# Three edits in a fused attention and mixture-of-experts kernel: operands of a late matmul stage swapped, experts in another order, one scaling on another engine

## The chip, the cores and the metric

The kernel runs on one core of a Trainium2 chip. The metric is the device time of one execution in microseconds. TensorE is called PE, VectorE DVE, ScalarE ACT, GpSimd POOL and SyncE SP, as in the profile. SP, ACT and POOL have queues on which they issue DMAs.

## The reference

Three layers follow one another. Matrices are float32; the kernel splits each operand into a high and a low part (`hi`, `lo`) and takes three matmuls for one product (`mm3`: hi·hi, hi·lo, lo·hi).

```python
# attention: 4 batches, 8 heads, 576 positions, 64 columns, causal with decay
attn = softmax(q @ k.T / 8 + cum[i] - cum[j], causal) ; x = attn @ v   # x: 2304 x 512
# mixture of experts: 8 experts, 512 -> 1024 -> 512
en = emb / (norm(emb) + 1e-6) ; logits = xn @ en.T / tau
e = argmax(logits) ; gate = softmax(logits)[e]
y[e == k] = gate * (relu(x[e == k] @ w1[k]) @ w2[k])
# second layer: 512 -> 3 x 768 -> 512
h = maximum(maximum(y @ m1, y @ m2), y @ m3) ; out = h @ mo
```

With the reference's inputs (seed 0) the eight experts get 360, 313, 312, 305, 292, 250, 244 and 228 tokens. The one with 305 has 232 of them in the first three batches, which makes it the third largest there.

## The kernel before

The order of the instructions on every engine is written out when the kernel is built: a list scheduler (`Sched`, line 146) takes tasks with an engine or a choice of engines, an assumed cost, dependences and a priority, and always emits the task that can begin first by its own estimates. Tasks hold buffers by name (`get`, `rel`). Each engine then works through its list in order, with semaphores between them. So an estimate changed in one place can move instructions in another.

**Attention** (`attention`, line 259) takes 16 pairs of heads in turn: scores, masked maximum on DVE, `exp` on ACT, transposes of the probabilities on PE, the product with v, and a matmul with `w144` (line 568) that also gives each head's share of the expert logits. `expert_rows` (line 112) makes the columns of `w144` from the scaled expert embeddings: a short chain over DVE and POOL for the norms (lines 118 to 127), a scaling of 8x512 on DVE (line 129), four transposes (line 133) and two copies (line 137). `route_batch` (line 779) picks the expert of each token of a batch. The 64 KB pieces of x go to `x_dram` by line 588; the last pair's pieces go out on SP's and ACT's queues in turn.

**The early expert.** After three batches `early_expert` (line 838) chooses the expert that is third by size so far (`SEAT`). Its first 256 tokens (`SOON`) are gathered, and `early_slot` (line 609) computes h = relu(x·w1) for them at the end of attention: eight chunks of 128 rows of w1, 12 matmuls of 256 columns each (`pe`, lines 679 to 698, called through `mm3`, lines 1172 to 1174), into three PSUM buffers. The weights w1 are loaded in four pieces (line 657), the third into a part of the v buffer, the fourth when the first's input tile is free. `square_sums` (line 939) runs five squares for each batch on ACT (line 943).

**The late tokens.** Up to 96 tokens (`LATE`) of that expert come from the last batch. `first_slot` (line 887) finds them, POOL gathers them (line 1336), PE transposes them (line 1343) and ACT and DVE split them (lines 1209 and 1354). In `moe` (line 1177), expert 0's pass over `hmm` then takes 96 matmuls with the weights as the stationary side and the 96 tokens as the moving side:

```python
for kc in range(KC):
    mm3(nc, ph[:, 0:C], w[0][:, kc, fs], w[1][:, kc, fs], X[k][0][:, kc, 0:C], X[k][1][:, kc, 0:C], kc == 0, kc == KC - 1)
```

The results go through relu (line 1406) and a subtraction (line 1411) into columns of the same h tiles (`g.he`). Then `ymm` multiplies h (340 columns) by w2 in 96 matmuls (`py`).

**The other experts.** `sort_experts` (line 975) sorts them by size, the early one first; slot k has room for `CAP[k]` tokens and is `CAP[k]` columns wide in both matmul stages (`ph`, `py`, 96 matmuls each). Its tokens are gathered in chunks of up to 128. Weights arrive in pieces of 512 KB (line 1239), are split by ACT (line 1209) and DVE (line 1226) and live in a ring of four. Beside the experts, weights of the second layer are decoded on DVE (lines 1269 to 1294). Tokens that don't fit a slot are done in a loop at the end of the program. The **second layer** works through 2304 columns in five chunks.

Of the kernel before, what the change touches and what calls it, by code (L numbers as in the profile page):

```python
# [19 lines left out]
DW = D + E  # L20
# [10 lines left out]
CAP = [340, 384, 338, 316, 298, 280, 264, 244]  # L31
# [6 lines left out]
NCOL = 24  # L38
CHUNKS = [(0, 384), (384, 512), (896, 512), (1408, 512), (1920, 384)]
# [72 lines left out]
def expert_rows(nc, g, sp, ps):  # L112
# [11 lines left out]
    nc.vector.scalar_tensor_tensor(out=ss[:, 2:3], in0=ss[:, 0:1], scalar=ss[:, 2:3], in1=ss[:, 1:2], op0=ALU.mult, op1=ALU.add)  # L124
# [3 lines left out]
    yield dict(eng="DVE", cost=0.65)  # L128
    nc.vector.tensor_scalar(out=e, in0=e, scalar1=ss[:, 3:4], scalar2=rt, op0=ALU.mult, op1=ALU.mult)
# [129 lines left out]
def attention(tc, g, qT, kT, v, x_dram, es):  # L259
# [266 lines left out]
    def pair_out(p):  # L526
# [63 lines left out]
        sd.task("SP", 3.2, store, u0, [fn_[p, 0], fn_[p, 1]], lat=2.0)  # L590
# [8 lines left out]
    def batch_out(b):  # L599
# [3 lines left out]
        last[0] = sd.chain(g.batch_done(b, lg), pr, deps + [last[0], consts_done] + ([part[0], part["pick"]] if b == B - 1 else []))  # L603
        sd.chain(g.square_sums(b, lambda: XL[b][:, :, :, 0:D]), pr + 40, deps + [consts_done])
# [4 lines left out]
    def early_slot(chosen):  # L609
# [6 lines left out]
        wdone, xdone, xhis, wl = [], [], [], []  # L616

        for c in range(SOON // 128):
# [26 lines left out]
            th = sd.task(("ACT", "DVE"), (act(512), dve(512)), xhi, 10 * NP + 15, [tr] + ready[NP - 1])  # L645
            xhis.append(th)
            xdone.append(sd.task("DVE", dve(512), xlo, 10 * NP + 15, [th], rel=[("s", ("xe", c))]))

        for q in range(4):
            def load(e, q=q):  # L650
                if not er:
                    er[0] = nc.sync.value_load(g.expi0[0:1, 0:1], min_val=0, max_val=E - 1)
                if q == 2:
                    raw[q] = V[0].rearrange("p a d -> p (a d)")[:, 0:1024]
                else:
                    raw[q] = flat(ld.tile([128, 2, S], F32, tag=("q2", "k2")[q % 2], name=f"we{q}"))[:, 0:1024]
# [11 lines left out]
            when = scores_of(NP - 3) if q < 2 else scores_of(NP - 2) + xhis + (late if q == 2 else [fn_[NP - 1, 1]])  # L668
            u = 10 * NP + (20, 21, 22, 31.2)[q]
            free = [chosen] + ready[NP - 2] if q < 2 else [chosen, fo[NP - 5]] if q == 2 else [wdone[1], xhis[0]]  # L670
            l = sd.task("SP", 1.5, load, 10 * NP - 12 + q, free, lat=3.0)
# [6 lines left out]
        for f in range(8):  # L678
            def mm(e, f=f):
                t = ph[f] = ps_s.tile([128, 512], F32, tag="s", name=f"pe{f}")  # L680
# [21 lines left out]
            m = sd.task("PE", 12 * (SOON + 31) / 2400, mm, u, [wdone[f // 2], fbs[NP - 1, 0], fbs[NP - 1, 1]] + xdone, get=("s", ("e", f)))  # L702
            th = sd.task(("ACT", "DVE"), (act(SOON), dve(SOON)), relu, u, [m])
            sd.task("DVE", dve(SOON), rest, u, [th], rel=[("s", ("e", f))])

    last, part, fbs = [None], {}, {}
# [19 lines left out]
    early_slot(part["pick"])  # L726
# [7 lines left out]
def routing_consts(nc, g, cp):  # L734
# [9 lines left out]
    g.iok = iota("iok", [128, E, E], [[1, E], [0, E]])  # L744
# [34 lines left out]
def route_batch(nc, g, b, lg, rp, ps):  # L779
# [22 lines left out]
                                   op1=ALU.is_equal)  # L802
    yield dict(eng="PE", cost=0.2, get=("o", ("pr", b)))
# [9 lines left out]
    if last:  # L813
        yield from first_slot(nc, g, b, pr, rp, ps)
        return
# [22 lines left out]
def early_expert(nc, g, cp, rp, ps):  # L838
    EE, ST = [128, E, E], [128, NCH, E]
    step, two = dict(eng="DVE", cost=0.24, kind="port"), dict(eng="DVE", cost=0.4, kind="port")  # L840
# [4 lines left out]
    yield two  # L845
    key = rp.tile([128, E], F32, tag="key", name="key3")
    nc.vector.scalar_tensor_tensor(out=key, in0=p3[:, 0:E], scalar=8.0, in1=g.w8[:, 1, :], op0=ALU.mult, op1=ALU.add)
    cnt = rp.tile([128, E], F32, tag="cnt", name="cnt3")
    nc.vector.tensor_copy(cnt, p3[:, 0:E])
    yield dict(eng="DVE", cost=0.24, kind="port", rel=[("o", "p3")])  # L850
    gt = rp.tile(EE, F32, tag="gt", name="gt3")
    nc.vector.tensor_tensor(out=gt, in0=key.unsqueeze(1).to_broadcast(EE), in1=key.unsqueeze(2).to_broadcast(EE), op=ALU.is_gt)
    yield two
    r = rp.tile([128, E], F32, tag="r", name="r3")
    nc.vector.tensor_reduce(out=r, in_=gt, op=ALU.add, axis=AX.X)
    g.ohe = cp.tile([128, E], F32, name="ohe")
    nc.vector.tensor_scalar(out=g.ohe, in0=r, scalar1=float(SEAT), scalar2=None, op0=ALU.is_equal)
    yield two
    ex = rp.tile([128, E], F32, tag="ex", name="ex")
    nc.vector.tensor_tensor(out=ex, in0=g.ohe, in1=g.ioe[:, 0, :], op=ALU.mult)  # L860
    g.expi0 = cp.tile([128, 1], I32, name="expi0")
    with low(reason="an expert's number, summed in float32, is a small whole number"):
        nc.vector.tensor_reduce(out=g.expi0, in_=ex, op=ALU.add, axis=AX.X)
    yield two
    tm = rp.tile(ST, F32, tag="tm", name="tm")
    nc.vector.tensor_tensor(out=tm, in0=g.tab.rearrange("p e c -> p c e"), in1=g.ohe.unsqueeze(1).to_broadcast(ST), op=ALU.mult)
    tab0 = rp.tile([128, NCH], F32, tag="tab0", name="tab0")
    nc.vector.tensor_reduce(out=tab0, in_=tm, op=ALU.add, axis=AX.X)
# [887 lines left out]
```

## Time and profile before

| what | value |
|---|---|
| three runs | 751.6, 751.2, 755.11 us; median 751.6 |
| profiled execution, its own time | 753.75 us |
| its span, first to last instruction | 752.0 us, so 1.75 us lie around it |
| granted PE clock, mean over the span | 0.983 of full speed |
| PE busy | 733.8 us (98%) |
| DVE, ACT, POOL busy | 445.0, 371.2, 143.6 us |

PE's busy time counts each matmul from its begin to its modelled end, and matmuls overlap; how fast PE works is read from the distance between two begins. [...]

### The profile page before, as it was taken

To read this page: it belongs to the slowest core of one execution; us is meant where nothing else is said; L and a number is where in the kernel's file an instruction comes from. 1 tells how busy PE (TensorE), PEld (TensorE's weight loads), DVE (VectorE), ACT (ScalarE), POOL (GpSimd) and SP (SyncE) were. 2 spreads that over 40 slices of the span, in tenths; PEclk is the share of its full clock that TensorE was granted. 3 is DMA by queue.
4 is the path that set the end of the run, shared out by engine and by line. 5 is a ranking of instruction groups with operands and counts; after the bars stand their busy time and mean duration, and the time that the engine had idled before them with its cause. 6 is when DMAs were issued, how large, how long until landed. Compare 5 with 4: busy or idle time off the path is not lost. (4 is left out here: it accounts for less than half of the span.)

```text
span 752.0 us, 13022 instructions
## 1 busy us (share of the span) xinstructions
PE 733.8 (98%) x4743; PEld 666.0 (89%) x4743; DVE 445.0 (59%) x1131; ACT 371.2 (49%) x850; POOL 143.6 (19%) x145
## 2 busy tenths in 40 slices
PE   8899999999999999999989999999999999999996
PEld 8788888887899999999989999988888888888995
DVE  8988878988755888888677879612212231221220
ACT  7689989988537554556555554411121121112111
POOL 6966364541011100110210000010020001001001
PEclk9999999999978999999999999999999999999999
DMA  7868657534434565556657543010010001001001
GB/s 250 252 185 253 190 159 192 137 88 145 140 113 141 176 202 197 194 169 236 225 170 233 167 160 128 13 43 1 0 43 14 1 15 42 1 1 42 15 1 44
DMA packets 44731, 89.78 MB, mean 119 GB/s; under 512 B 23280, under 2 KB 23280, under 8 KB 44664
## 3 DMA queue, kind: packets, MB, share of 16 engines
q1 hardware_dynamic: 40536, 78.97, 33.8%
q0 software_dynamic: 3552, 9.80, 3.7%
q8 instruction: 39, 0.64, 0.4%
q14 instruction: 28, 0.23, 0.1%
q10 hardware_dynamic: 576, 0.15, 0.1%
HBM read 74.89 MB, written 9.44 MB: 112 GB/s over the span
## 5 line engine op out<-in xcount | busy, mean ns | idle before, releaser
L1526 DVE TENSOR_TENSOR tm<-pm,tm 128x512 f32<-128x512 f32 (+1 forms) x60 | 38.3, 638 | 184.6 <-PE pm L1174 184.5
L1172 PE MATMUL pm<-y,m 128*128 128x512 f32 (+1 forms) x288 | 109.4, 380 | 0.0
L1173 PE MATMUL pm<-y,m 128*128 128x512 f32 (+1 forms) x288 | 109.4, 380 | 0.0
L1174 PE MATMUL pm<-y,m 128*128 128x512 f32 (+1 forms) x288 | 109.4, 380 | 0.0
L466 ACT ACTIVATE P<-P,nm 128x576 f32<-128x576 f32 (+2 forms) x144 | 83.6, 584 | 6.4 <-DVE nm L442 5.0
L1226 DVE TENSOR_TENSOR w<-stg,w 128x1024 fp32r<-128x1024 f32 x60 | 73.3, 1221 | 19.5 <-ACT w L1209 19.1
L1568 POOL DMA_INDIRECT out_dram<-oo,ctidx x18 | 17.8, 987 | 336.6 <-ACT oo L1565 333.6
L1209 ACT ACTIVATE g<-tm 128x512 fp32r<-128x512 f32 (+1 forms) x30 | 17.7, 589 | 118.4 <-DVE tm L1526 118.4
L1209 ACT ACTIVATE w<-stg 128x1024 fp32r<-128x1024 f32 x58 | 61.0, 1055 | 27.4 <-issue 9.8
L1172 PE MATMUL py<-h,w 128*128 128x384 f32 (+6 forms) x224 | 69.4, 310 | 0.0
L1174 PE MATMUL py<-h,w 128*128 128x384 f32 (+6 forms) x224 | 68.3, 305 | 0.0
L1173 PE MATMUL py<-h,w 128*128 128x384 f32 (+6 forms) x224 | 68.2, 305 | 0.0
L1172 PE MATMUL ph<-x,w 128*128 128x384 f32 (+6 forms) x224 | 67.9, 303 | 0.0
L1173 PE MATMUL ph<-x,w 128*128 128x384 f32 (+6 forms) x224 | 67.6, 302 | 0.0
L1174 PE MATMUL ph<-x,w 128*128 128x384 f32 (+6 forms) x224 | 67.6, 302 | 0.0
L414 PE MATMUL s<-R,At 128*128 128x288 f32 (+3 forms) x170 | 60.6, 370 | 3.1 <-DVE nm L442 1.2
L1172 PEld LDWEIGHTS pm<-y,m 128*128 128x128 f32 x288 | 54.2, 188 | 9.4
L1173 PEld LDWEIGHTS pm<-y,m 128*128 128x128 f32 x288 | 54.2, 188 | 9.4
L1174 PEld LDWEIGHTS pm<-y,m 128*128 128x128 f32 x288 | 54.2, 188 | 9.4
L442 DVE CUSTOM_DVE_ANT_0 P<-s,mask 128x288 f32<-128x288 f32 (+3 forms) x128 | 58.3, 475 | 3.2 <-PE s L420 1.4
L1336 POOL DMA_INDIRECT gat<-x_dram,gidx x21 | 23.4, 1116 | 190.0 <-PE xt L1343 148.2
L485 PE MATMUL t<-ident,P 128*128 128x128 f32 x320 | 56.7, 277 | 0.8 <-ACT PT L524 0.3
(369 smaller groups left out, 1799.5 us busy)
## 6 DMA issues: line engine op xcount, KB each, us to landing
stg<-in_w_dram SPq DMA_DIRECT2D x60, 512.0 KB
sd<-in_m_dram SPq DMA_DIRECT2D x18, 512.0 KB
q<-in_q_dram SPq DMA_DIRECT2D x15, 576.0 KB
k<-in_k_dram SPq DMA_DIRECT2D x15, 576.0 KB
Bt<-At SPq DMA_DIRECT2D x15, 288.0 KB
V<-in_v_dram SPq DMA_DIRECT2D x4, 1024.0 KB
x_dram<-XL SPq DMA_DIRECT2D x62, 64.0 KB
sd_o<-in_mo_dram SPq DMA_DIRECT2D x6, 512.0 KB
```

What stands on the lines that cost most here:

```text
L414: nc.tensor.matmul(st[:, 0:wp], lt[0:kk, r, q0:q0 + 128], rt[0:kk, r, j0:j0 + wp], start=(ps_i == 0), stop=(p > 0 and ps_i == 1))
L442: nc.vector.tensor_tensor_reduce(out=P[0:n, j0:j0 + w], in0=st_.pop((h, t, k))[0:n, 0:w], in1=g.mask[0:n, m0:m0 + w], scale=-0.125, scalar ...
L466: nc.scalar.activation(out=P[0:n, 0:ext], in_=P[0:n, 0:ext], func=AF.Exp, bias=nm[0:n, k:k + 1], scale=-1.0, accum_out=sums[b][0:n, t, c:c ...
L485: nc.tensor.transpose(w[:, 128 * a:128 * a + 128], P[:, 128 * a:128 * a + 128], g.ident)
L1172: nc.tensor.matmul(out, whi, xhi, start=start, stop=False)
L1173: nc.tensor.matmul(out, whi, xlo, start=False, stop=False)
L1174: nc.tensor.matmul(out, wlo, xhi, start=False, stop=stop)
L1209: nc.scalar.activation(out=out, in_=in_, func=AF.Copy)
L1226: ENG[e].tensor_tensor(out=w[:, 1], in0=t, in1=w[:, 0].bitcast(F32), op=ALU.subtract)
L1336: nc.gpsimd.indirect_dma_start(out=t[0:n], out_offset=None, in_=x_dram, in_offset=bass.IndirectOffsetOnAxis(ap=idx, axis=0))
L1526: nc.vector.tensor_tensor(out=mx[0], in0=mx["p", w][:, 0:MC], in1=mx[0], op=ALU.max)
L1568: nc.gpsimd.indirect_dma_start(out=out, out_offset=bass.IndirectOffsetOnAxis(ap=g.sidx[:, col:col + 1], axis=0), in_=o[1], in_offset=None, ...
```

## The change

The first expert's pass over h gets code of its own, `late_rows`: in four quarters of 256 columns of w1, the 96 tokens are the stationary side and the weights the moving side, 12 matmuls a quarter. The result stands tokens by columns, so each quarter goes through relu, two transposes on PE, a copy and a subtraction into the h tiles. `CAP` is in another order, with 256 where 264 was, and `RANK` says which size belongs to which slot. The expert rows are scaled on ACT with one factor, and one step of their norm is a `tensor_scalar`. At the end of attention: the last pair's five stores all go out on SP; the last batch's squares follow the third early chunk; the early chunks alternate between two PSUM pools (five buffers) and their relu is always on ACT; the third and fourth weight pieces go into a spare `XL` tile; `early_expert`'s counts become a task of their own (`early_count`), and the late tokens' ids (`late_ids`) are made ahead of the ranks' matmuls. A gather's assumed cost and delay are 1.27 and 2.9 for 1.04 and 2.4; sorting waits for the first half of the token split alone.

```diff
-CAP = [340, 384, 338, 316, 298, 280, 264, 244]
+CAP = [340, 338, 256, 384, 244, 316, 280, 298]
+RANK = [0] + [1 + sorted(CAP[1:], reverse=True).index(c) for c in CAP[1:]]
# expert_rows
-    nc.vector.scalar_tensor_tensor(out=ss[:, 2:3], in0=ss[:, 0:1], scalar=ss[:, 2:3], in1=ss[:, 1:2], op0=ALU.mult, op1=ALU.add)
+    nc.vector.tensor_scalar(out=ss[:, 2:3], in0=ss[:, 0:1], scalar1=ss[:, 2:3], scalar2=ss[:, 1:2], op0=ALU.mult, op1=ALU.add)
...
-    yield dict(eng="DVE", cost=0.65)
-    nc.vector.tensor_scalar(out=e, in0=e, scalar1=ss[:, 3:4], scalar2=rt, op0=ALU.mult, op1=ALU.mult)
+    nc.vector.tensor_scalar(out=rt, in0=rt, scalar1=ss[:, 3:4], scalar2=None, op0=ALU.mult)
+    yield dict(eng="ACT", cost=0.65)
+    nc.scalar.activation(out=e, in_=e, func=AF.Copy, scale=rt)
# attention
-                (nc.scalar if p == NP - 1 and t % 2 else nc.sync).dma_start(out=dst[r0:r0 + ROWS[t]], in_=X[0:ROWS[t], t])
+                nc.sync.dma_start(out=dst[r0:r0 + ROWS[t]], in_=X[0:ROWS[t], t])
-                if q == 2:
-                    raw[q] = V[0].rearrange("p a d -> p (a d)")[:, 0:1024]
+                if q > 1:
+                    if q == 2:
+                        raw["x"] = xl.tile([128, NBLK, H, DW], F32, tag="XL", name="spare").rearrange("p t h c -> p (t h c)")
+                    raw[q] = raw["x"][:, 1024 * (q - 2):1024 * (q - 1)]
-                t = ph[f] = ps_s.tile([128, 512], F32, tag="s", name=f"pe{f}")
+                t = ph[f] = (ps_t if f % 2 else ps_s).tile([128, 512], F32, tag="st"[f % 2], name=f"pe{f}")
-            th = sd.task(("ACT", "DVE"), (act(SOON), dve(SOON)), relu, u, [m])
+            th = sd.task("ACT", act(SOON), relu, u, [m])
+    sd.chain(g.square_sums(B - 1, lambda: XL[B - 1][:, :, :, 0:D]), 10 * NP + 60, [mains[2]])
# routing_consts
-    g.iok = iota("iok", [128, E, E], [[1, E], [0, E]])
+    g.iok = cp.tile([128, E, E], F32, name="iok")
+    for k in range(E):
+        nc.gpsimd.memset(g.iok[:, k], float(RANK[k]))
# moe
-            ga = sd.task("Pool", 1.04, gather, use - 12, deps, get=("scr", (k, c)), lat=2.4)
+            ga = sd.task("Pool", 1.27, gather, use - 12, deps, get=("scr", (k, c)), lat=2.9)
-    sorted_ = sd.chain(sort_experts(nc, g, g.cp, rp, ps_o), 6.0, [g.placed] + xdone[0])
+    sorted_ = sd.chain(sort_experts(nc, g, g.cp, rp, ps_o), 6.0, [g.placed, xhi[0, 0]])
+    def late_rows(use, deps):
+        for q in range(4):
+            t0 = use + mms(12, 256) * q
+            def lmm(e, low, q=q):
+                if not low:
+                    po[q] = ps_h.tile([128, 512], F32, tag="y", name=f"pl{q}")
+                w = [t.rearrange("p (k f) -> p k f", k=KC) for t in g.we[q]]
+                for kc in range(KC):
+                    x = X[0][low][:, kc, 0:LATE]
+                    for i in range(2 - low):
+                        nc.tensor.matmul(po[q][0:LATE, 0:256], x, w[i][:, kc, :], start=(low == 0 and kc == i == 0), stop=(low == 1 and kc == KC - 1))
...
+            def lflip(e, q=q):
+                pt[q] = ps_h.tile([128, 512], F32, tag="y", name=f"ptl{q}")
+                for i in range(2):
+                    nc.tensor.transpose(pt[q][:, 128 * i:128 * i + LATE], hl[q][0:LATE, 0, 128 * i:128 * i + 128], g.ident[0:LATE, 0:LATE])
...
+            m = sd.task("PE", mms(8, 256), lambda e, fn=lmm: fn(e, 0), t0, [xhi[0, 0]], get=("y", ("l", q)))
+            m = sd.task("PE", mms(4, 256), lambda e, fn=lmm: fn(e, 1), t0, [m] + deps)
+            r = sd.task(("ACT", "DVE"), (act(256), dve(256)), lrelu, t0 - 1, [m], rel=[("y", ("l", q))])
+            x = sd.task("PE", 0.22, lflip, t0 + mms(12, 256) * 1.5, [r], get=("y", ("lt", q)))
...
     for k in range(E):
-        C = CAP[k] if k else LATE
+        C = CAP[k]
+        if k == 0:
+            h_lo, h_pe = late_rows(now, xdone[0])
+            now += mms(48, 256) + 0.9
-        for f in range(FC):
+        for f in range(FC if k else 0):
```

## Rows read from the trace of the kernel before

**Rows 1.** The page, busy PE and granted clock in 40 slices of the span.
```profile
PE   8899999999999999999989999999999999999996
PEclk9999999999978999999999999999999999999999
```
**Rows 2.** Stretches: us, each engine's busy us (instructions), clock, DMA share, GB/s.
```profile
208.70:227.30 18.60, 17.88 (x114) 17.65 (x112) 11.03 (x36) 6.36 (x13) 2.85 (x3) 0.65 0.31 100
...
245.70:444.00 198.30, 196.40 (x1420) 194.97 (x1419) 157.82 (x267) 110.29 (x184) 15.40 (x14) 0.99 0.61 201
```
**Rows 3.** Timeline of PE, 205 to 228 us: begin, length, operation, [idle before, releaser].
```profile
205.97 0.28 PE L1172 MATMUL pe<-xs,R 128*128 128x256 f32 x1
...
208.69 0.49 PE L1343 MATMUL xt<-ident,gat 96*128 96x96 f32 x4
209.02 0.27 PE L984 MATMUL pn<-oh,ones 128*128 128x8 f16 x5
...
209.77 0.31 PE L1172 MATMUL ph<-x,At 128*128 128x96 f32 x1 [0.45 <-ACT x L1209]
210.36 0.31 PE L1173 MATMUL ph<-x,At 128*128 128x96 f32 x1 [0.28 <-DVE x L1354]
...
227.29 0.62 PE L1172 MATMUL py<-At,w 128*128 128x340 f32 x1
```
**Rows 4.** Stretches of one us around the clock's fall and rise.
```profile
214.00:215.00 1.00, 1.00 (x13) 1.00 (x12) 1.00 (x1) 0.25 (x1) 0.00 (x0) 0.67 0.69 283
...
230.00:231.00 1.00, 1.00 (x5) 1.00 (x5) 0.32 (x3) 0.00 (x0) 0.00 (x0) 0.50 0.67 111
231.00:232.00 1.00, 1.00 (x7) 1.00 (x6) 0.00 (x0) 0.00 (x0) 0.00 (x0) 0.80 0.94 381
```
**Rows 5.** Timelines of ACT and DVE: a relu, a subtraction, a weight piece's subtraction.
```profile
208.89 0.38 ACT L693 ACTIVATE hv<-pe 128x256 fp32r<-128x256 f32 x1 [0.98 <-PE pe L1174]
```
```profile
220.12 0.26 DVE L1411 SCALAR_TENSOR_TENSOR Bt<-ph,At 128x96 f32 x1 [0.54 <-ACT At L1406]
...
227.98 1.22 DVE L1226 TENSOR_TENSOR w<-stg,w 128x1024 fp32r<-128x1024 f32 x1
```
**Rows 6.** POOL's gathers: timeline, and from line 1336 their landing times, 190 to 250.
```profile
221.34 0.95 POOL L1336 DMA_INDIRECT gat<-x_dram,gidx  x1 [0.30 <-issue]
```
```profile
DMA to landing us min/median/max: 3.5/5.7/10.1
```
**Rows 7.** Tile ph on PE, 208 to 250: durations in ns, first and last begin.
```profile
L1172 PE MATMUL ph<-x,w x9: 334/334/420, 245.7 to 249.9; 128*128 128x384 f32 x9
```
**Rows 8.** End of attention: a stretch of one us, and ACT's timeline.
```profile
202.00:203.00 1.00, 0.51 (x8) 0.30 (x6) 0.96 (x3) 0.98 (x4) 0.00 (x0) 1.00 0.61 238
```
```profile
196.28 2.02 ACTq L588 DMA_DIRECT2D x_dram<-XL  x2
198.35 0.63 ACT L943 ACTIVATE sq<-XL 128x512 f32<-128x512 f32 x1 [4.45 <-DVE oh L801]
```
**Rows 9.** The expert rows: timelines of DVE and PE, and one stretch.
```profile
27.09 1.18 DVE L124 SCALAR_TENSOR_TENSOR ess<-ess 8x1 f32<-8x1 f32 x1
28.30 0.14 DVE L125 TENSOR_SCALAR ess<-ess 8x1 f32<-8x1 f32 x1
...
28.72 2.29 DVE L129 TENSOR_SCALAR emb<-emb,ess,rt 8x512 f32<-8x512 f32 x1
```
```profile
31.07 0.41 PE L133 MATMUL pe<-ident,emb 8*128 8x8 f32 x4 [1.26 <-DVE emb L129]
```
```profile
33.00:37.00 4.00, 4.00 (x22) 3.97 (x21) 3.08 (x12) 2.17 (x7) 3.78 (x5) 0.57 0.47 161
```
**Rows 10.** Slot 6's third chunk: PE's timeline, and two stretches after it.
```profile
394.54 0.41 PE L1343 MATMUL xt<-ident,gat 8*128 8x8 f32 x4 [1.91 <-DVE x L1354]
```
```profile
395.00:399.00 4.00, 4.00 (x20) 4.00 (x21) 2.56 (x6) 1.00 (x3) 0.00 (x0) 0.57 1.00 269
...
400.00:410.00 10.00, 10.00 (x86) 10.00 (x85) 6.93 (x12) 7.36 (x14) 0.00 (x0) 1.00 0.48 152
```

More of the change, by code (lines that the diff above doesn't have):

```diff
@@ L701, in early_slot @@
             u = 10 * NP + 30 + 0.4 * f
-            m = sd.task("PE", 12 * (SOON + 31) / 2400, mm, u, [wdone[f // 2], fbs[NP - 1, 0], fbs[NP - 1, 1]] + xdone, get=("s", ("e", f)))
-            th = sd.task(("ACT", "DVE"), (act(SOON), dve(SOON)), relu, u, [m])
-            sd.task("DVE", dve(SOON), rest, u, [th], rel=[("s", ("e", f))])
-    last, part, fbs = [None], {}, {}
+            m = sd.task("PE", 12 * (SOON + 31) / 2400, mm, u, [wdone[f // 2], fbs[NP - 1, 0], fbs[NP - 1, 1]] + xdone, get=("st"[f % 2], ("e", f)))
+            th = sd.task("ACT", act(SOON), relu, u, [m])
+            sd.task("DVE", dve(SOON), rest, u, [th], rel=[("st"[f % 2], ("e", f))])
+            mains.append(m)
+        return mains
+    last, part, fbs, sq, stores = [None], {}, {}, {}, {}
     split_tasks(1)
@@ L725, in attention @@
             part["pick"] = sd.chain(g.choose(), 10 * NP - 35, [last[0]])
-    early_slot(part["pick"])
+        if p == NP - 2:
+            part["count"] = sd.chain(g.count(), 10 * NP + 16, [part["pick"], fo[p]])
+    mains = early_slot(part["pick"], [sq[B - 2], fn_[NP - NPAIR, 0]] + [stores[p] for p in range(NP - 2 * NPAIR, NP - NPAIR)])
+    sd.chain(g.square_sums(B - 1, lambda: XL[B - 1][:, :, :, 0:D]), 10 * NP + 60, [mains[2]])
     sd.run()
@@ L802, in route_batch @@
                                    op1=ALU.is_equal)
+    if last:
+        yield dict(eng="DVE", cost=0.5)
+        r0 = late_ids(nc, g, b, rp)
     yield dict(eng="PE", cost=0.2, get=("o", ("pr", b)))
@@ L813, in route_batch @@
     if last:
-        yield from first_slot(nc, g, b, pr, rp, ps)
+        yield from first_slot(nc, g, b, pr, r0, rp, ps)
         return
@@ L839, in early_expert @@
     EE, ST = [128, E, E], [128, NCH, E]
-    step, two = dict(eng="DVE", cost=0.24, kind="port"), dict(eng="DVE", cost=0.4, kind="port")
+    step = dict(eng="DVE", cost=0.22, kind="port")
     low = nc.allow_low_precision
@@ L899, in first_slot @@
                             in1=g.idv[:, b, :].unsqueeze(2).to_broadcast([128, NBLK, 2]), op=ALU.mult)
+    return r0
+def first_slot(nc, g, b, pr, r0, rp, ps):
+    sl = slice(NBLK * b, NBLK * b + NBLK)
+    SH, SL = [128, NBLK, E], [128, NBLK, LATE]
+    oh = g.oh[:, sl, :]
+    low = nc.allow_low_precision
     yield dict(eng="DVE", cost=1.3)
@@ L1372, in moe @@
     mkeys = [(w, j) for j in range(3) for w in range(3)] + [("o", j) for j in range(3)]
-    total = now + mms(96, LATE) + mms(96, CAP[0]) + sum(mms(192, n) for n in CAP[1:])
+    total = now + mms(48, 256) + 0.9 + mms(96, CAP[0]) + sum(mms(192, n) for n in CAP[1:])
     begin = now
@@ L1387, in hmm @@
             def hmm(e, f=f, q=q, k=k, C=C):
-                w = [(weight[1, k, q][:, i] if k else g.we[q][i]).rearrange("p (k f) -> p k f", k=KC) for i in range(2)]
+                w = weight[1, k, q].rearrange("p s (k f) -> p s k f", k=KC)
                 ph = hh["p", k, f] = ps_h.tile([128, 512], F32, tag="y", name=f"ph{k}_{f}")
@@ L1410, in rest @@
-            def rest(e, f=f, k=k, C=C):
-                nc.vector.scalar_tensor_tensor(out=cols("DVE", k, f, 1, C), in0=hh["p", k, f][:, 0:C], scalar=0.0,
-                                               in1=cols("DVE", k, f, 0, C).bitcast(F32), op0=ALU.max, op1=ALU.subtract)
-            pe_ = sd.task("PE", mms(12, C), hmm, t0, ([wsplit[key]] if k else []) + xdone[k] + yall, get=("y", ("h", k, f)),
-                          rel=[("ring", key)] if f % 2 and k else [])
+                ht = hp.tile([128, 2, PADW], F32R, tag=f"h{f}", name=f"h{k}_{f}")
@@ new lines, in relu @@
+                hh[k, f] = ht[:, 0], ht[:, 1]
+                ph = hh["p", k, f]
+                if e == "ACT":
+                    nc.scalar.activation(out=ht[:, 0, 0:C], in_=ph[:, 0:C], func=AF.Relu)
+                else:
+                    nc.vector.tensor_scalar(out=ht[:, 0, 0:C], in0=ph[:, 0:C], scalar1=0.0, scalar2=None, op0=ALU.max)
+            def rest(e, f=f, k=k, C=C):
+                ht, ph = hh[k, f], hh["p", k, f]
+                nc.vector.scalar_tensor_tensor(out=ht[1][:, 0:C], in0=ph[:, 0:C], scalar=0.0,
+                                               in1=ht[0][:, 0:C].bitcast(F32), op0=ALU.max, op1=ALU.subtract)
@@ L1709, in main @@
             g.batch_done = lambda b, X: route_batch(nc, g, b, X, rp, g.ps_o)
+            g.count = lambda: early_count(nc, g, cp, rp)
             g.choose = lambda: early_expert(nc, g, cp, rp, g.ps_o)
```

104 lines of the change are left out of this document (62 added, 42 removed).

## The prediction

> **What bounds the kernel now.** I read the page first. PE is busy in nearly every slice, and its granted clock sags in three places [rows 1]. So PE's list sets the end, and a change pays where it shortens that list, fills a gap in it or lifts the clock. The stretches come next: the one with the late tokens' stage ran at a mean clock of 0.65, while the 198 us of the other experts hold 198.30 - 196.40 = 1.9 us of idle PE in all [rows 2]. PE's timeline then shows the stage itself: the late tokens' transposes begin at 208.69, the first of 96 matmuls at 209.77, the first `py` at 227.29 [rows 3]. That is 17.52 us for 96 matmuls of 96 columns. Early matmuls of 256 columns go every (208.69 - 205.97)/24 = 0.113 us [rows 3]; at that pace the 96 would be done in 10.9 us. The rest is the clock: it falls between 214 and 215, stands at 0.50 (1.2 GHz) until 231 and rises between 231 and 232, after 340-column matmuls have run for 4 us [rows 4]. PE was idle for 18.60 - 17.88 = 0.72 us of that stretch, all of it before 210.4 [rows 2, 3]; what it did before the fall was a stream of short matmuls. The other two sags follow idle time: the wait for the expert rows at 31 us [rows 9] and the wait of slot 6's third chunk at 394 us [rows 10].
>
> **The late stage.** The 96 matmuls go; 48 of 256 columns and eight transposes take their place. Four transposes take 209.02 - 208.69 = 0.33 us [rows 3]. So PE's own work is 48 x 0.113 + 2 x 0.33 = 6.1 us, and 0.2 for the sort's small matmuls that stand inside the stage in both kernels: 6.3 us. The price that is not plain is the round trip: a quarter's transposes wait for its relu, and `py` for the copy and the subtraction behind them. One trip costs 0.28 until a matmul has landed, 0.38 for the relu, 0.28 for the transposes, 0.26 for the copy and as much for the subtraction [rows 3, 5] = 1.46 us. The priority puts a quarter's transposes half a quarter behind the next one's matmuls, and `py` begins with quarter 0, so the last trip lies under `py` of quarters 0 to 2. The cover fails where ACT is inside the cast of a weight piece when a relu falls due; the subtraction of such a piece takes 1.22 us on DVE [rows 5]. Bounds: 6.3 us with every trip hidden, 6.3 + 4 x 1.46 = 12.1 us with none. The nearer case is the early chunks, whose relu and subtraction run under the next chunk; I allow 1 us and take 7.3. Gain 17.5 - 7.3 = 10.2 us (5.4 to 11.2).
>
> The clock. If the short stream made it fall, it holds now: 256 columns in 0.113 us are as dense as the early chunks, which had 1.00. Then `py` gets back what it lost from 227.3 to 232, half of 3.7 us and a fifth of one [rows 3, 4], 2.05 us (0 if it falls again).
>
> The junction. PE idled 0.45 and 0.28 us for the split of the late tokens [rows 3]. The ids are now made ahead of the ranks, three DVE steps fewer in the chain to the gather. On the other side all five stores of the last pair queue on SP, some 1 us each by ACT's two in 2.02 [rows 8], and the gather waits for them to land, as SP's first loads of w2 stand behind them. The loads have slack, since `py` wants them 7 us after the junction. I take 0.3 us of 0 to 0.7.
>
> **The end of attention.** In the us from 202 PE was busy for 0.51 [rows 8]. The fourth and fifth early chunk had to wait for a PSUM buffer, whose relu stood on ACT behind 2.02 us of issuing stores and behind squares of 0.63 us; the ranks' last matmuls waited there too. Five buffers, no stores on ACT and later squares can give back up to that 0.5 us. Against it, five squares, some 3 us, now lie among the later chunks' relus, between which ACT idled 0.98 us [rows 5, 8], and one can hold up the late tokens' split by its 0.63 us. I take a gain of 0.4 (from 0.5 down to a loss of 0.6). The third and fourth weight piece come earlier and bring their casts and subtractions to where DVE is full; PE's list hides them, and without that cover half a piece is 0.6 us, the same bound. The seven DVE steps of `early_count` leave the chain to the first gathers; nobody waits for them until the ranks.
>
> **The expert rows.** The 8x1 step took 1.18 us and the scaling 2.29 us on DVE, where an 8x1 `tensor_scalar` took 0.14; ACT takes 0.63 us for 512 columns [rows 8, 9]. The step becomes a `tensor_scalar`, the scaling goes to ACT, one more 8x1 step is added: 1.18 + 2.29 - 2 x 0.14 - 0.14 - 0.63 = 2.4 us off the chain, more than PE's wait of 1.26 us [rows 9]. Behind the wait the clock lost 4 x (1 - 0.57) = 1.7 us. Of both I take 1.0 and 1.0, since the scheduler lays attention out anew from here and DVE's queue may be late with the two copies that follow: 2.0 us (0 to 3.0; a loss of 0.6 if the step only holds up an `exp` on ACT). Eight memsets for one `iota` are setup on POOL that nothing near waits for; priced like DVE's 0.14 they are 1 us under PE's attention list.
>
> **The order of the slots.** The widths are the same but 256 for 264. At 264 columns PE begins 86 matmuls in 10 us [rows 10], 0.116 each against 0.113: 192 x 0.003 = 0.6 us. A slot of 256 has no third chunk: its four transposes go, 0.3 us, and so do the wait of 1.91 us ahead of them and the sag behind, 4 x (1 - 0.57) = 1.7 us [rows 10]. That wait came where three narrow slots follow one another and DVE has the least time for its work on each; wide and narrow slots alternate now, and the plan counts a gather as later. But new boundaries can have waits of their own: I put half of one with its sag against it, 1.8 us. Net 0.6 + 0.3 + 1.9 + 1.7 - 1.8 = 2.7 us (from 4.5 down to a loss of 2.7, two such waits).
>
> **Sum.** 10.2 + 2.05 + 0.3 + 0.4 + 2.0 + 2.7 = 17.7 us off the profiled execution's own 753.75 (a span of 752.0 and 1.75 around it): 736.1. That execution lay 2.15 us above the median of the runs; from the median, 751.6, the sum gives 733.9. I forecast 735.0, between them.
>
> **The rivals.** *Given back at the next expert.* Slot 1's matmuls began at 245.7 [rows 7]; the terms ahead of them ask for them 13 us earlier, at 232.7. Their tokens hang on the sort, which ran on DVE inside the old stage. The third gather began at 221.34, took 0.95 us and a median of 5.7 us to land [rows 6]; then 0.33 for transposes, 0.63 for a cast and 0.6 for a subtraction: 229.6. DVE has five subtractions of 0.26 and two of 1.22 us [rows 5] to fit in sooner; all ahead of the sort they make it 233.3, and a landing of 10.1 us makes it 237.7, a wait of 5 us. For it: DVE was busy for 11.03 of 18.6 us there [rows 2]. Against: the late case needs both. Time 740. Chance 0.15.
>
> *The clock falls again.* Were the idle at the junction its cause, it would fall 4.3 us into the new stage as into the old: the last 3 us double, and `py` loses its 2 us, 740 as well. Against: after the gap at 202 the clock held. Chance 0.09. [...]
>
> *Nothing is hidden.* ACT is too late each time, every quarter's trip lies open, and the idle brings a sag: 735 + 4.8 + 1.7 = 741.5. Then the swap would still gain, as the old stage ran mostly at half speed. Chance 0.07.
>
> *Slower.* Each change of slot brings a wait as at 394 us, since the next slot's transposes wait for a PSUM buffer that DVE frees late. Wait and sag are 3.6 us, and half of one is in the sum: all seven give 735 - 1.8 + 25.2 = 758. With six, 755, the kernel is still within half a per cent of 751.6, about what a measurement of it can tell from no change. The old order had one in seven. Chance 0.03. The slots themselves hold: the sixth largest of the seven others has 244 tokens for the 256.
>
> **Numbers.** The forecast has 0.61, with a range of its own from 729 to 739 (all gains whole are 22 us, 729.6 from the median). The three rivals about 740 count as faster too; 0.05 is left for edits that cancel. So faster by over 0.5% (below 747.8): 0.92, within it 0.05, slower 0.03. The range reaches from 729 to 742.5, over the three rivals, and leaves out the last two cases and the tails.
>
> **What will show it.** PE's timeline: 48 matmuls 0.113 us apart, the first `py` some 7 to 8 us behind the first of them in place of 17.5, and a clock of 1.00 through both. Little idle ahead of slot 1. No wait at the expert rows and no sag behind it. No transposes of eight tokens. It would be wrong if PE idles at slot boundaries, if the new transposes wait for ACT, or if attention itself grew longer in its new layout.

## The result, and the profile after

The kernel takes 744.15 us (median of 20 runs), before it was 751.62 us (20 runs): a ratio of 0.9908, 95% interval 0.9885 to 0.9931. It is faster, by 7.5 us (0.9%) in place of the forecast 16.6, and the time lies above the predicted range, which ended at 742.5.

The profiled execution of the changed kernel took 750.11 us, 6 us above its median: its clock stood at 0.50 from 29 to 38 us, where eleven of the 14 other kernels below with the new expert rows have 1.00 in their profiles. So its spans from the late transposes on are compared, not its total.

PE's busy share and granted clock in 40 slices of the span:
```profile
PE   9899999999987999999989999999999999999996
...
PEclk9799999999998999999999999999999999999999
```
The clock's 7 in the 12th slice [rows 1] is gone, an 8 in the 13th has stayed, and the second slice has a 7 of its own. In the 12th and 13th slice PE itself falls to 8 and 7: there it waits.

The clock is the share of full speed that PE was granted. PE's timeline before shows what it does to the pace: the `py` of 340 columns begin every (230.82 - 227.98)/10 = 0.284 us at 0.50, and every (233.85 - 232.01)/12 = 0.153 us at 1.00. The first is 340/284 = 1.2 columns a ns, and as that estimate the prediction's 1.2 GHz can be read.
```profile
227.98 0.49 PE L1174 MATMUL py<-At,w 128*128 128x340 f32 x1
...
230.82 0.49 PE L1172 MATMUL py<-At,w 128*128 128x340 f32 x1
...
232.01 0.32 PE L1172 MATMUL py<-At,w 128*128 128x340 f32 x1
...
233.85 0.32 PE L1172 MATMUL py<-At,w 128*128 128x340 f32 x1
```

Three stretches hold the sags (us, each engine's busy us, clock, DMA share, GB/s):
```profile
236.00:243.00 7.00, 3.85 (x16) 3.88 (x17) 0.50 (x1) 0.90 (x2) 0.94 (x1) 0.52 0.53 178
29.00:38.00 9.00, 9.00 (x41) 8.27 (x41) 5.08 (x18) 5.98 (x18) 5.28 (x5) 0.50 0.71 181
212.00:216.00 4.00, 3.56 (x24) 3.47 (x25) 2.91 (x8) 3.37 (x5) 0.00 (x0) 0.57 0.02 5
```
PE's timeline, to hold against [rows 3, 7]: the late tokens' transposes, the first `pl` of the new stage, the first `py`, then slot 1's three chunks of tokens and its first `ph`:
```profile
211.94 0.52 PE L1378 MATMUL xt<-ident,gat 96*128 96x96 f32 x4 [1.69 <-DMA gat<-x_dram,gidx]
...
213.04 0.53 PE L1426 MATMUL pl<-At,x 128*96 128x256 f32 x1 [0.45 <-ACT x L1244]
...
220.72 0.40 PE L1207 MATMUL py<-At,w 128*128 128x340 f32 x1
...
230.22 0.60 PE L1378 MATMUL xt<-ident,gat 128*128 128x128 f32 x4
...
231.59 0.60 PE L1378 MATMUL xt<-ident,gat 128*128 128x128 f32 x4
...
239.15 0.78 PE L1378 MATMUL xt<-ident,gat 82*128 82x82 f32 x4 [5.12 <-DMA gat<-x_dram,gidx]
...
244.47 0.40 PE L1207 MATMUL ph<-x,w 128*128 128x338 f32 x1
```
The stage from `pl` to `py` takes 220.72 - 213.04 = 7.7 us in place of 17.5, near the forecast 7.3, although its clock is not the 1.00 that was forecast: it stands at 0.57 from 212 to 216. Then more is lost: slot 1's third chunk is flipped at 239.15, after 5.12 us of waiting for its gather, and with the clock at 0.52 behind it `ph` begins at 244.47. From `py` to `ph` it is 23.8 us where before it was 18.4. And the late transposes themselves waited 1.69 us for their gather, which [rows 3] doesn't show.

POOL's timeline, the gathers:
```profile
206.87 0.93 POOL L1371 DMA_INDIRECT gat<-x_dram,gidx  x1 [25.69 <-DVE Bt L703]
223.59 0.96 POOL L1371 DMA_INDIRECT gat<-x_dram,gidx  x1 [15.79 <-ACT hv L1244]
224.84 1.76 POOL L1371 DMA_INDIRECT gat<-x_dram,gidx  x1 [0.30 <-issue]
226.91 1.40 POOL L1371 DMA_INDIRECT gat<-x_dram,gidx  x1 [0.31 <-issue]
```
The three of slot 1 begin at 223.59, 224.84 and 226.91; the last is 82 rows, and its issue takes 1.40 us in place of 0.95 [rows 6]. Its rows are flipped 12.2 us after it began. SP's queue, what its instructions waited for (in all, times, longest):
```profile
SPq L1274 <- ACT sq L978: 3.8, 1, 3.8
```
One of the weight loads (line 1274) waited 3.8 us for `sq`, the squares of the last batch; it and the next went out from 206.99 on, in the microsecond of the late gather. SP's timeline:
```profile
206.99 0.88 SPq L1274 DMA_DIRECT2D stg<-in_w_dram  x2
```

The expert rows are off the chain: their scaling on ACT took 0.71 us and PE no longer waits for it [rows 9]. A wait for a DMA (`Bt<-At`) ahead of them grew to 2.1 us (1.2 before). ACT's timeline, and PE's waits of the first 60 us:
```profile
30.91 0.71 ACT L131 ACTIVATE emb<-emb,rt 8x512 f32<-8x512 f32 x1
```
```profile
PE s L416 <- DMA Bt<-At: 2.1, 1, 2.1
```
From slot 1's first `ph` to the second layer's first matmul it is 441.48 - 244.47 = 197.0 us against 445.24 - 245.66 = 199.6. That is near the 2.7 us that the order was to give, but kernels with the old order come as low: 196.3 in x1_late and x4_attn below. And a wait like that of slot 6 [rows 10] has come back at a later change of slot, for a chunk of 24 rows:
```profile
386.85 0.42 PE L1378 MATMUL xt<-ident,gat 24*128 24x24 f32 x4 [2.05 <-DVE x L1389]
```
So the late stage, the big term, came as worked out, and the loss is in two places: the third gather of slot 1, and the late gather.

### The profile page after: what moved, and what is told of

Same layout as the page of the kernel before. It is cut to its first block, busy times and chain, and to the rows that moved or that the text cites. A ratio compares the mean times of both kernels' runs of the same rounds, so it can differ in the third digit from the quotient of the medians.

```text
span 748.0 us, 12944 instructions
## 1 busy us (share of the span) xinstructions
PE 724.8 (97%) x4699; PEld 656.7 (88%) x4699; DVE 439.6 (59%) x1125; ACT 374.2 (50%) x859; POOL 145.0 (19%) x151
## 5 line engine op out<-in xcount | busy, mean ns | idle before, releaser
L1207 PE MATMUL py<-h,w 128*128 128x338 f32 (+6 forms) x224 | 68.4, 305 | 0.9 <-DVE h L1492 0.9
L1207 PE MATMUL ph<-x,w 128*128 128x338 f32 (+6 forms) x224 | 67.7, 302 | 0.0
L1208 PE MATMUL ph<-x,w 128*128 128x338 f32 (+6 forms) x224 | 67.3, 301 | 0.0
L1208 PE MATMUL py<-h,w 128*128 128x338 f32 (+6 forms) x224 | 67.3, 301 | 0.0
L1209 PE MATMUL ph<-x,w 128*128 128x338 f32 (+6 forms) x224 | 67.2, 300 | 0.0
L1209 PE MATMUL py<-h,w 128*128 128x338 f32 (+6 forms) x224 | 67.2, 300 | 0.0
```

The lines of the kernel that those rows point to most:

```text
L1207: nc.tensor.matmul(out, whi, xhi, start=start, stop=False)
L1208: nc.tensor.matmul(out, whi, xlo, start=False, stop=False)
L1209: nc.tensor.matmul(out, wlo, xhi, start=False, stop=stop)
```

## The experiments

Gains are against the kernel before on the same chip: 752.27 us beside the four parts, 751.09 beside x5 to x8, 751.87 beside x9, x10, x12 and x13, 752.5 beside x14 to x17, 753.85 beside x18 and x19.

**The four parts alone.** Each part of the diff is put on the kernel before by itself.

x1_late: `late_rows` in place of the `ph<-x,At` loop, the gather's assumed cost, the sort's shorter dependence; the old `CAP`.
```diff
+            h_lo, h_pe = late_rows(now, xdone[0])
-        for f in range(FC):
+        for f in range(FC if k else 0):
```


> The swapped late stage alone (with the gathers' assumed costs), all else as before. If the gain is given back at slot 1 because its third gather lands late: the stage itself is 9 to 11 us shorter, PE then waits 3 to 7 us for slot 1's tokens with a sag of the clock behind, and the time falls by 5 to 7 us. If the wait in the changed kernel comes from the new order of slots or from the end of attention instead: no wait over 1 us ahead of slot 1, and the time falls by 11 to 12 us.

x2_order:
```diff
-CAP = [340, 384, 338, 316, 298, 280, 264, 244]
+CAP = [340, 338, 256, 384, 244, 316, 280, 298]
```


> The new order and sizes of the slots alone. By the prediction's sum: 2.7 us less (0.9 of work, the wait at 394 us and its sag gone, half a new one). By the rival that new boundaries wait as the old one did: 0 to 1 us less, with one wait of about 2 us at a later change of slot.

x3_rows:
```diff
+    nc.scalar.activation(out=e, in_=e, func=AF.Copy, scale=rt)
```


> The expert rows scaled on ACT alone. By the prediction's sum: 2 us less, no wait for the rows at 31 us. By the rival that the wait only moves to a DMA or to another engine at the same place: no difference beyond 1 us, with a sag of the clock in the first 40 us as before.

x4_attn: everything else, so the stores on SP, the squares behind the third early chunk, two PSUM pools, the counts as a task, the ids ahead of the ranks.
```diff
+                nc.sync.dma_start(out=dst[r0:r0 + ROWS[t]], in_=X[0:ROWS[t], t])
+    sd.chain(g.square_sums(B - 1, lambda: XL[B - 1][:, :, :, 0:D]), 10 * NP + 60, [mains[2]])
```


> The edits at the end of attention alone (stores on SP, five PSUM buffers, squares later, spare tile, counts and ids apart). By the prediction's sum: 0.4 to 0.7 us less. By the rival that the late tokens are gathered later (their index waits on PE's list, the stores on SP): PE waits 1 to 2 us for them, and the time is 0 to 2 us more.

Measured: 737.71 us (0.9791, 0.976 to 0.9822), 750.15 (0.996, 0.9938 to 0.9981), 749.93 (0.9958, 0.993 to 0.9986), 755.65 (1.0044, 1.0018 to 1.007). Gains of 14.6, 2.1 and 2.3 us and a loss of 3.4: 15.6 in all, of which the change as a whole keeps 7.5. Two things were now plain. The end of attention costs; and up to 8 us are lost only when the parts meet. Up to, because the parts share a gain: before, PE waited 1.91 us for slot 6's third chunk [rows 10]; in the profiles of x1_late, x2_order and x4_attn it doesn't, and in x3_rows it hardly does, so the sum may count that wait and its sag several times:
```profile
392.32 0.41 PE L1344 MATMUL xt<-ident,gat 8*128 8x8 f32 x4 [0.38 <-DVE x L1355]
```
In the new stage alone PE waits for nothing but the split of the late tokens, 0.45 us; tile by tile, `pl`, `py` and slot 1's `ph` on PE (durations in ns, first and last begin):
```profile
L1391 PE MATMUL pl<-At,x x16: 279/282/357, 209.7 to 214.5; 128*96 128x256 f32 x16
```
```profile
L1172 PE MATMUL py<-At,w x12: 316/316/404, 216.4 to 227.6; 128*128 128x340 f32 x12
```
```profile
L1172 PE MATMUL ph<-x,w x32: 334/334/420, 233.1 to 249.3; 128*128 128x384 f32 x32
```
The stage is 216.4 - 209.7 = 6.7 us and `py` to `ph` 16.7, with a clock of 1.00 throughout. With the end of attention alone, PE's waits from 195 to 262 us begin with the late gather:
```profile
PE xt L1374 <- DMA gat<-x_dram,gidx: 1.8, 1, 1.8
```

**Which parts clash.** The change without the edits at the end of attention (x7_noattn), and the stage with them but in the old order (x8_moeattn).

> The changed kernel with the edits around the end of attention taken back: it keeps the late tokens as the stationary side, the mixed order of size and the scaling of the expert rows on ScalarE. Theory A (the edits at the end of attention cost 3.4 us alone and bring on the late gather of the expert at slot 1): the three other edits were worth 14.6, 2.1 and 2.3 us alone, so together about 733 us (731 to 736), no wait of PE for gat at slot 1, clock 1.00 between 210 and 250. Theory B (the mixed order is what clashes with the new late stage): 741 us or more and PE waits 3 us or more for gat ahead of slot 1 here too.

> The kernel before with the new late stage and the edits around the end of attention, old order of sizes and old scaling of the expert rows. Theory A (the clash is between the late stage and the end of attention): about 746 us (744 to 749), a wait of 3 us or more for gat at slot 1 with the clock at 0.5 behind it. Theory B (the clash needs the mixed order): 741 us, the sum of 14.6 gained and 3.4 lost, and no wait at slot 1.

Measured: 743.52 us (0.9909, 0.9877 to 0.9941) and 739.36 (0.9843, 0.9812 to 0.9875). My theory A fell: the clash needs the order, not the end of attention. Without the latter PE waits all the same; POOL's third gather and the flip that waits for it:
```profile
219.10 1.40 POOL L1340 DMA_INDIRECT gat<-x_dram,gidx  x1 [0.30 <-issue]
```
```profile
230.95 0.78 PE L1347 MATMUL xt<-ident,gat 82*128 82x82 f32 x4 [4.73 <-DMA gat<-x_dram,gidx]
```
Here the gather goes out 12.9 us behind the stage's first matmul (13.9 in the changed kernel) and is flipped 11.9 us after it began. With the old order the third gather has 128 rows, goes out at 224.09 and is flipped 7.0 us later with no wait:
```profile
224.09 0.94 POOL L1367 DMA_INDIRECT gat<-x_dram,gidx  x1 [0.30 <-issue]
```
```profile
231.04 0.60 PE L1374 MATMUL xt<-ident,gat 128*128 128x128 f32 x4
```

**Earlier, or fewer chunks.** On the changed kernel, the sort ahead of the weight pieces' subtractions (x5_sort), or 256 tokens at slot 1 (x6_slot1):
```diff
-    sorted_ = sd.chain(sort_experts(nc, g, g.cp, rp, ps_o), 6.0, [g.placed, xhi[0, 0]])
+    sorted_ = sd.chain(sort_experts(nc, g, g.cp, rp, ps_o), -10.0, [g.placed, xhi[0, 0]])
```
```diff
-CAP = [340, 338, 256, 384, 244, 316, 280, 298]
+CAP = [340, 256, 338, 384, 244, 316, 280, 298]
```


> The changed kernel with one number altered: the chain that sorts the experts has priority -10 instead of 6, so VectorE takes it ahead of the late stage's low parts. Theory A (the late sort is the cause of slot 1's wait): gidx by 219 instead of 222.6, the wait of 5.1 us and the sag of about 3.4 us behind it go, late stage longer by up to 1 us: 736 to 738 us. Theory C (the third gather is slow because the weight loads fill the DMA engines between 227 and 238, whenever it is issued): the gathers go out 3 us earlier but a wait of 3 us or more stays: 741 to 744 us.

> The changed kernel with the sizes of slots 1 and 2 exchanged (256 tokens at slot 1, two gathers of 128 rows instead of three). Theory A (it is the third gather alone that is late): no wait ahead of slot 1, 736 to 739 us, if slot 2's three gathers are in time behind a shorter slot 1. Theory C (the gathers are slow because of the loads beside them): the second lands late instead, a wait of 2 us or more stays, 741 to 744 us.

Measured: 740.43 us (0.9862, 0.9835 to 0.989) and 736.25 (0.9808, 0.978 to 0.9836). The earlier gather is in time, though it still takes 8.2 us to land; but the late stage grew to 8.5 us and the subtraction of the second chunk held up the third by 2.5 us, so half of the gain is spent. Without a third chunk at slot 1 there is no wait. Both fit a late sort as well as a slow gather; the next runs separate them.

**The gather itself.** 96 rows for 82 (x9_rows16; `n` is the rows gathered, the flip still takes 82):
```diff
+                n = -(-n // 16) * 16
                 idx = g.gidx[0:n, k, c:c + 1] if k else g.gidx0[0:n, c:c + 1]
```


> The changed kernel with each gather of a part chunk made longer, to the next multiple of 16 rows (82 to 96 rows at slot 1; the rows added are read and not used). Theory D (a gather of 82 rows is slow by itself: it took 8 to 12 us to its flip in three kernels where gathers of 128 rows at the same place took 7 us or less): the wait of 5 us ahead of slot 1 falls under 1 us, 736 to 739 us. Theory A/C (it is late because it is issued late, or because weight loads fill the DMA engines): 17% more bytes help nothing, the wait stays 4 us or more, 742 to 745 us.

Measured: 737.02 us (0.9801, 0.9766 to 0.9836). More bytes, and 7 us less. The gather goes out at 225.76, 15.0 us behind the stage's first matmul and so later in it than in the changed kernel (13.9), and its rows are flipped at 232.72 without a wait; the issue takes 0.91 us:
```profile
225.76 0.91 POOL L1372 DMA_INDIRECT gat<-x_dram,gidx  x1 [0.30 <-issue]
```
```profile
232.72 0.45 PE L1379 MATMUL xt<-ident,gat 82*128 82x82 f32 x4
```
So it was the 82 rows. The kernel before had the same gather at slot 2, the third in POOL's timeline from 239 on, with a median landing for it alone of 10.1 us:
```profile
243.01 2.36 POOL L1336 DMA_INDIRECT gat<-x_dram,gidx  x1 [1.49 <-PE xt L1343]
```
```profile
gat<-x_dram,gidx POOLq DMA_INDIRECT x1, 10.1
```
That is the 10.1 of [rows 6]: not the tail of a spread, but this one gather.

Beside it the other cost was tried. One edit taken back, half of the stores on ACT (x12_stores):
```diff
-                nc.sync.dma_start(out=dst[r0:r0 + ROWS[t]], in_=X[0:ROWS[t], t])
+                (nc.scalar if p == NP - 1 and t % 2 else nc.sync).dma_start(out=dst[r0:r0 + ROWS[t]], in_=X[0:ROWS[t], t])
```


> The changed kernel with one edit at the end of attention taken back: half of the last pair's stores go out from ACT's queue again. Theory E (all ten stores on SP's queue push the weight loads behind them into the flight of the late gather, whose landing went from 3.3 to 4.9 us): the weight loads begin 3 us earlier, the wait of 1.7 us for the late gather goes, time 1.5 to 2.5 us below the changed kernel, 742 us. Rival (the late gather is late because the matmul that gives its rows comes later in PE's order): the wait of 1.7 us stays, 744 us.

Measured: 744.34 us (0.9912, 0.9884 to 0.994), and a wait of 1.76 us for the late gather. Theory E fell: the first load went out earlier, but the next still waited 4.7 us for `sq`:
```profile
SPq L1274 <- ACT sq L978: 4.7, 1, 4.7
```

Without the edits at the end of attention and with 256 tokens at slot 1 (x10_slot1_noattn), and the same with part chunks gathered in multiples of 16 rows (x13_both):

> The changed kernel without the edits at the end of attention, and with 256 tokens at slot 1 and 338 at slot 2. If the 82 rows at slot 1 were the whole clash, the gains of the three other edits add up: 733 us (731 to 735), no wait of PE at the late gather or at slot 1. If the clash is with anything else in the new order: 738 us or more.

> As the run before it, with part chunks gathered in multiples of 16 rows as well. If gathers of part chunks wait nowhere else on the path: the same time within 1 us, 733 us. If they also cost at the later slots: 730 to 732 us.

Measured: 734.81 us (0.9766, 0.9734 to 0.9797) and 735.01 (0.9772, 0.9738 to 0.9805). With the clash gone the gains nearly add up (17.1 of 14.6 + 2.1 + 2.3 = 19.0 us), and slow gathers further on lie under other work, though there is an even slower one, the 116 rows of slot 4 (POOL's timeline, and its landing):
```profile
266.86 1.26 POOL L1340 DMA_INDIRECT gat<-x_dram,gidx  x1 [0.31 <-issue]
```
```profile
gat<-x_dram,gidx POOLq DMA_INDIRECT x1, 11.8
```

**What is slow in 82.** `n = max(n, 88)`, and 90, 84, 86, on the changed kernel:

> The changed kernel with gathers of part chunks of at least 88 rows (82 becomes 88; 88 = 8 x 11, and not a multiple of 16). Theory D1 (only a multiple of 16 rows is quick): the wait of 4 to 5 us ahead of slot 1 stays, issue on GpSimd 1.3 us or more, 743 us. Theory D2 (any multiple of 8, or any size near 96, is quick): the wait goes, 737 us.

> The same with 90 rows (2 x 45). D1: the wait of 4 to 5 us stays, 743 us. D2, multiples of 8: stays as well, 743 us; D2, size alone: the wait goes, 737 us.

> The changed kernel with gathers of part chunks of at least 84 rows (82 becomes 84). 96, 90 and 88 rows were quick, 82 slow, and 116 rows at a later slot landed in 11.8 us. Theory D3 (quick where the number of rows has a divisor near 16: 96 has 16, 90 has 15, 88 has 11, 84 has 14, while 82 has 2 and 116 has 4): quick, a wait ahead of slot 1 under 1 us, 738 to 741 us. Theory D4 (a size limit between 82 and 88 rows): undecided, wait either 4 us or none.

> The same with 86 rows (2 x 43, no divisor from 3 to 16). Theory D3: slow as 82 are, an issue of 1.3 us or more on GpSimd, a wait of 4 to 5 us ahead of slot 1, the gathers of slot 2 behind it landing in 9 us, 742 to 745 us. Theory D4: if 84 rows are quick, 86 are as well: no wait, 738 to 741 us.

Measured: 739.19 us (0.9814, 0.9769 to 0.986), 740.94 (0.9857, 0.9802 to 0.9912), 739.64 (0.9808, 0.9753 to 0.9864), 746.32 (0.9891, 0.9835 to 0.9947). My first idea, multiples of 16, fell with 88 and 90; 84 quick and 86 slow settles it. The third gather with 84 rows, its landing, and the flip:
```profile
222.22 0.95 POOL L1372 DMA_INDIRECT gat<-x_dram,gidx  x1 [0.31 <-issue]
```
```profile
gat<-x_dram,gidx POOLq DMA_INDIRECT x1, 7.0
```
```profile
229.37 0.48 PE L1379 MATMUL xt<-ident,gat 82*128 82x82 f32 x4
```
and with 86:
```profile
224.24 1.43 POOL L1372 DMA_INDIRECT gat<-x_dram,gidx  x1 [0.30 <-issue]
```
```profile
gat<-x_dram,gidx POOLq DMA_INDIRECT x1, 10.9
```
```profile
235.24 0.78 PE L1379 MATMUL xt<-ident,gat 82*128 82x82 f32 x4 [3.49 <-DMA gat<-x_dram,gidx]
```

| rows gathered | largest divisor up to 16 | issue on POOL, us | landing, us | PE's wait for it, us |
|---|---|---|---|---|
| 82 (changed kernel) | 2 | 1.40 | 12.2 to the flip; landing 7.1 in x2_order, 8.2 in x5_sort; at slot 2 8.8 in x1_late, 10.1 before | 5.12 |
| 84 | 14 | 0.95 | 7.0 | none |
| 86 | 2 | 1.43 | 10.9 | 3.49 |
| 88 | 11 | 0.98 | 7.7 | 0.72 |
| 90 | 15 | 0.95 | 7.3 | 0.29 |
| 96 | 16 | 0.91 | 6.1 (in x16_sq) | none |

In these six sizes the time doesn't go with the size but with the divisor: where it is 11 or more the issue took 0.91 to 0.98 us and the landing 6.1 to 7.7, and 86 rows took 1.43 and 10.9. The packets in the traces go the same way: the 82 rows of x5_sort and the 84 of x18_rows84 both go as 42 packets of data, the first from 220.5 to 226.0 with at most three in flight at once, the second from 226.1 to 228.4 with up to eleven. The gathers' queue, with its share of 16 engines' time, in x5_sort from 221.5 to 225.5 and in x18_rows84 from 226.0 to 226.6:
```profile
q0 software_dynamic: 36, 0.15, 11.4%
```
```profile
q0 software_dynamic: 42, 0.11, 46.7%
```
11.4% of 16 engines is 1.8 of them, 46.7% is 7.5. So I take it, as an estimate from packets and shares, that about two engines carry 82 rows and some four times as many (7.5 to 1.8) carry 84; why the divisor should decide that, no run shows. What else moves may count as well: 82 rows landed in 7.1 us in x2_order, where all DMA together took 0.19 of the engines' time from 224 to 229, and in 8.2 us in x5_sort, with 0.89 from 221.5 to 225.5.

**The squares.** x9_rows16 with the last batch's squares put back behind its rows (x16_sq), and that with 256 tokens at slot 1 (x17_sq_slot1):
```diff
-        if b < B - 1:
-            sq[b] = sd.chain(g.square_sums(b, lambda: XL[b][:, :, :, 0:D]), pr + 40, deps + [consts_done])
+        sq[b] = sd.chain(g.square_sums(b, lambda: XL[b][:, :, :, 0:D]), pr + 40, deps + [consts_done])
-    sd.chain(g.square_sums(B - 1, lambda: XL[B - 1][:, :, :, 0:D]), 10 * NP + 60, [mains[2]])
```


> The changed kernel with 96 rows in the third gather, and with the square sums of the last batch put back to where they stood (behind the last pair's rows, not behind the third early chunk). Theory F (the weight loads of slot 0 wait for these square sums, 4 us longer than before, so that they go out in the same microsecond as the late gather and slow its landing from 3.3 to 4.9 us): the second and third weight loads go out 2 us or more ahead of the late gather, the wait of 1.7 to 2.0 us for it falls under 0.5 us, 735 us against 737. Rival (the early chunks just end sooner than the gather can land): the wait stays over 1.5 us and so does the time, 737 us.

> As the run before it, with 256 tokens at slot 1 and 338 at slot 2. If nothing else of the edits at the end of attention costs: 733 to 735 us, as the kernel without those edits (734.8). If another of them costs: 736 us, as with them (736.3).

Measured: 734.75 us (0.9767, 0.9733 to 0.9802) and 733.6 (0.9753, 0.9718 to 0.9787), the lowest of all, though not told apart from each other. The intervals of x9_rows16 and x16_sq overlap; their traces are what tells them apart. With the squares back three loads go out at 197, the late gather of 201.29 lands in 3.7 us (5.3 in x9_rows16), PE's wait for it falls from 2.02 to 0.43, and the stage from 8.8 us to 6.7 with the clock at 1.00. PE's timeline of x9_rows16, then SP's and PE's of x16_sq:
```profile
209.31 0.87 PE L1379 MATMUL xt<-ident,gat 96*128 96x96 f32 x4 [2.02 <-DMA gat<-x_dram,gidx]
```
```profile
197.09 1.51 SPq L1272 DMA_DIRECT2D stg<-in_w_dram  x3
```
```profile
205.10 0.52 PE L1377 MATMUL xt<-ident,gat 96*128 96x96 f32 x4 [0.43 <-DMA gat<-x_dram,gidx]
```

## Why the prediction was wrong

**The late stage** was right: 10.2 forecast, 17.5 - 7.7 = 9.8 in the changed kernel's profile and 10.8 where nothing disturbs it (6.7 us). **The clock on `py`** was right too: 1.7 us alone for 2.05. The rival that laid the old fall on the junction's idle doesn't hold by itself: from 203 to 212 us x16_sq idles 9.00 - 8.12 = 0.88 us, before it was 0.72, and its clock stays at 1.00. Behind a longer wait it can fall: of the ten kernels with the new stage that wait some 1.7 us or more for the late gather, eight then lose clock (0.69 from 210 to 220 us in x9_rows16), and two don't (1.00 through the stage in x6_slot1 and x8_moeattn).

**The expert rows**: 2.0 forecast, 2.3 measured alone. The wait for them is gone, but x3_rows' own profile doesn't put the gain there. Its clock still sags (0.62 from 29 to 38 us, 0.81 before), slot 1's first `ph` comes only 0.7 us earlier (244.97 for 245.66), and 2.8 us come after it, up to the second layer (196.8 for 199.6), where slot 6's wait is shorter though the edit changes nothing there. So the size is in part luck. Its stretch:
```profile
29.00:38.00 9.00, 9.00 (x49) 8.33 (x48) 5.83 (x22) 6.71 (x20) 7.13 (x6) 0.62 0.57 168
```
Only the whole set of profiles speaks for the forecast that the sag would go: from 29 to 38 us the clock is 1.00 in eleven of 15 kernels with the new rows, and in one of five with the old. **The order**: 2.7 forecast, 2.1 alone. Its mechanism is not shown: the wait at slot 6 goes in kernels with the old order as well, and the changed kernel has one of 2.05 us at another slot, with no sag behind it (1.00 from 386 to 399 us).

**The end of attention** was the first failed step: a gain of 0.4 (loss of 0.6 at most) was forecast and a loss of 3.4 measured alone. I priced the moved squares by ACT's queue, where one could hold up a relu by 0.63 us, and took SP's loads to have slack. What waited was SP: two weight loads stood until the last square was done, so they were sent into the flight of the late gather. PE's wait for it, 1.7 to 2.3 us in every kernel with this edit in its place, and the sag that mostly followed were in no term. The gain was misread as well. PE's idle in the us from 202 [rows 8] was no wait for a PSUM buffer; PE's timeline before puts it down to DVE's `ohl`, the late tokens' one-hot:
```profile
202.79 0.38 PE L914 MATMUL p<-r,ohl 128*96 128x2 f16 x5 [0.49 <-DVE ohl L909]
```
That wait is gone in the changed kernel, but even in x16_sq the gather's 0.43 us stand in its place, so no run shows the junction's 0.3 us for the ids. The stores that I held against it cost nothing (x12_stores).

**Given back at the next expert** is what came, and it got a chance of 0.15. That the late case needs both, a later sort and a landing of 10.1 us, was right: with the sort early (x5_sort) or the gather quick (x9_rows16) the wait for it goes. The failed step is the chance, which took 10.1 us as the tail of a spread over gathers of one kind. The rows were there to be told apart: the before trace's only 82-row gather of that stretch is the one that took 10.1, and the change moves just these 338 tokens to slot 1, where the least time is. The later sort came in nearly every layout: the third gather began 12.9 to 15.1 us behind the stage's first matmul with the new stage (10.1 in x5_sort), before 221.34 - 209.77 = 11.6 us. That the forecast wait, 5 us, met the measured 5.12 is in part luck: the working adds the issue's 0.95 us to a landing that holds it already (x18_rows84's gather is issued at 222.22, lands after 7.0 and is flipped at 229.37). And the price left out the sag behind that wait, 7.00 x (1 - 0.52) = 3.4 us: 740 plus 3.4 is 743.4, against 744.15 measured, though the 3.8 us of the end of attention are not in it.

A small misreading: [rows 1] shows one sag of the clock and not three; the other two stand in [rows 9, 10] alone.

With both removed, and the rest of the change as it is, the kernel takes 734.75 us; the forecast was 735.0, though not term by term: the new stage alone gave 14.6 us, of which slot 6 holds a part, for 10.2 + 2.05. From 744.15, 7.1 us are the gather of 82 rows (x9_rows16) and, by the medians, 2.3 the squares.

**Open**: the packets carry no engine's number, so that the 82 rows lie on two engines is an estimate from packets in flight, the queue's share and six sizes. Why the clock from 29 to 38 us stood at 0.50 in one profile and at 1.00 in others with the same expert rows, and why some waits of some 2 us bring a sag and others don't, was not tried.

## What to carry to other kernels

Before a spread of landing times is priced, split it by shape: the worst may be one transfer, and the change may move just that one to where it counts. Try a gather with a few rows too many, so that a number near 16 divides them: at slot 1 here 84, 88, 90 and 96 rows landed in 6.1 to 7.7 us and 86 in 10.9, and with two rows more than 82 PE's wait of 5.12 us was gone. When work is moved later, ask of every queue, DMA issue included, who waits for the memory that it uses. And ask of a wait on the path what a sag behind it would cost: 3.4 us behind 5.12 here, and none behind another of 2.05.

## What was not expected of the hardware

A gather of 86 rows took 10.9 us to land and one of 84 rows 7.0 at the same place. In the changed kernel what stood behind the slow gather was late as well: the 128-row gather issued at 231.10 landed after 9.4 us, where the one ahead of the slow gather took 5.6. Its last packets, from 238.5 to 241, go at most two at a time.
```profile
gat<-x_dram,gidx POOLq DMA_INDIRECT x1, 9.4
```
